# A 2048-point convolution and an MLP on one core: right-angle twisted transform with uniform tables, operands laid out by the host, and one list schedule for the whole kernel

## The chip, the cores and the metric

The program runs on one core of one Trainium2 chip. The metric is device time in microseconds (us) of one execution. Most executions of one kernel here lie within about 1% of its median; each run is classed as fast or slow by its time. The profile is one execution; its span is somewhat shorter than the time measured for the same run (238.2 and 240.03 us for the changed kernel).

PE is the matmul engine, PEld its weight load, DVE the vector engine, ACT the activation engine, POOL the general-purpose engine, SP the engine whose queue issues nearly all DMAs. PE writes its results into PSUM; an evacuation is the copy of such a result to SBUF, the memory that the other operands lie in, by DVE or ACT. `kv` is also called u.

## The reference, cut to what matters

```
x = A_q                                    # (2048, 512), bf16
q = layernorm(x)
kv = shift4(A_k, A_shift_k) * A_v          # 4-tap causal filter per channel, times v
y  = causal_conv(kv, A_ssm_k) + kv * A_ssm_D   # 2048-tap filter per channel, by FFT in fp32
h  = x + q * y
b  = layernorm(h)
h1 = gelu(layernorm(b) @ w1)               # 512 -> 512
x1 = b + shift_tokens(h1, -1, +1, -2, +2 by quarter of the channels) @ w2
out = h + x1 + gelu(layernorm(x1) @ w3) @ w4   # 512 -> 1792 -> 512
```

Both kernels compute the convolution as matmuls, in two steps of a Cooley-Tukey transform each way. Step 1 multiplies with small 32-row tables; an exchange between partitions (DMA, SBUF to SBUF) follows; step 2 has one table for each of 16 slices; the product of the two spectra is taken slice by slice; then the two inverse steps follow, with a second exchange between them. So the work has a neck: no token of `h` exists before the last slice of the inverse's first half has been exchanged. Below, "the transform" is all before that, "the norm stage" is the stretch after it in which layer norms, w1 and w2 work their way in, and "the MLP" is the rest (w3 and w4).

## The kernel before

The filter comes as (channel, time) and is transposed on PE; k is transposed by DMA; the transform's order is written by hand, and only what follows it is ordered by the list scheduler (`Plan`). This simulates the kernel with an estimated duration for each task: of the tasks that are ready it takes the one that can start first, at a tie the one of higher priority, and puts it on the engine that ends it first where there is a choice. The priorities are searched for in 40 rounds.

```
    for c in range(DC):
        nc.sync.dma_start(hnat[:, c, :], A_ssm_k[c * P:(c + 1) * P, :])
    for c in range(DC):
        nc.sync.dma_start_transpose(kT[:, c, 16:KW], k_r[:, c * P:(c + 1) * P])
    ...
    for c in range(DC):                    # 64 transposes of the filter, 8 evacuations
        for bh in range(2):
            pt = ps_c.tile([P, 8, P], BF16, name="pt", tag="pk")
            for j in range(8):
                nc.tensor.transpose(pt[:, j, :], hnat[:, c, 8 * bh + j:S:16], ident[:])
            evac(xh[:, 8 * bh:8 * bh + 8, c * P:(c + 1) * P], pt[:], 1024, ...)
    ...
    for bl in range(NL):                   # filter: step 1, exchange
        for h in range(4):
            step1([xh[:, 4 * bl + bq, :] for bq in range(4)], zch, bl, h)
        exchange(zh, zch, bl)
    for g in range(2):
        nc.sync.dma_start(q_sb[:, 8 * g:8 * g + 8, :], q_r[:, 8 * g:8 * g + 8, :])
    ...
    for b in range(NB):                    # by hand: shift, step 1 of kv, step 2 of the filter, q statistics
        xk[b] = shift(b)                   # 16 matmuls of 128 columns, then DVE: times v
        if b >= 4:
            bl, h = divmod(b - 4, 4)
            step1([xk[4 * bl + bq][:] for bq in range(4)], zck, bl, h)
            if h == 3:
                exchange(zk, zck, bl)
        if b >= 6:
            spectrum(ng)                   # step 2 of the filter: 4 matmuls and an evacuation
            ng += 1
        if b in (9, 13):
            tables(b // 4)                 # PE transposes of the inverse's tables
        if b >= 4:
            qstat(b - 4)
    ...
    for i in range(NH + 2):                # step 2 of kv, products, inverse's first half
        if i < NH:
            prs[i] = fwd(i)
        if i >= 2:
            inv(i - 2, prs[i - 2])
    ...
    plan = Plan(...)                       # from here on a list schedule: inverse's second half,
                                           # norms, w1, w2, w3 (pieces of 512 tokens), w4
```

## Time and profile before

| | us | read from |
|---|---|---|
| time, median of 2 runs | 268.1 | runs |
| transform, to the first 32-row inverse matmul | 109.1 | chain of waits |
| from there to the first matmul of w3 | 48 | instructions of w3's line: first at 156.9 |
| w3, w4 and the rest | 110 | the rest of the span |

The page of the kernel before: the busy line, and the span in 40 slices of 6.7 us (a digit is the busy share in tenths, PEclk the clock granted to PE).

```profile
span 266.8 us, 4530 instructions
PE 231.9 (87%) x1803; PEld 119.0 (45%) x1803; DVE 161.9 (61%) x323; ACT 143.3 (54%) x202; POOL 54.1 (20%) x101
...
PE   8665957999579988665988999999999999999994
...
DVE  7986807669927998299999994898022250013322
ACT  3638152788479998266867856556500046632000
...
PEclk9999995999959999796899999999999999999999
```

From the 24th slice on PE is full and its clock whole. Before that PE is not full for long; DVE is, from the 18th to the 24th slice (the norm stage). The same as a table of stretches; the columns are the stretch, its length, then for PE, PEld, DVE, ACT and POOL the busy us and in brackets the instructions, then granted clock, DMA share and GB/s.

```profile
0.00:40.00 40.00, 28.12 (x342) 17.57 (x343) 27.06 (x51) 19.64 (x21) 8.35 (x28) 1.00 0.98 313
40.00:80.00 40.00, 33.50 (x383) 19.37 (x384) 27.55 (x54) 27.01 (x33) 3.15 (x2) 0.84 0.28 110
80.00:109.00 29.00, 24.69 (x186) 7.44 (x182) 25.47 (x37) 26.46 (x29) 2.44 (x4) 0.97 0.47 168
109.00:157.00 48.00, 39.22 (x361) 24.36 (x362) 41.59 (x103) 31.76 (x55) 30.86 (x52) 0.90 0.24 86
157.00:268.00 111.00, 106.41 (x537) 50.24 (x534) 40.20 (x79) 38.42 (x65) 9.30 (x15) 0.99 0.06 20
```

In the first 80 us DVE and ACT, which empty every matmul's result out of PSUM, are each busy between half and 70% of the time. The chain of waits (start, length, what) says why around 40 us: the exchange of the filter, then the load of q queued behind it, then DVE's statistics of q, and behind those, in DVE's own order, the work that PE waits for.

```profile
26.56 6.07 DMA rd<-rc
...
32.65 7.34 DMA q_sb<-in_A_q_dram
...
40.01 0.70 DVE qst L414
...
41.55 1.86 PE pk L406 x16
...
105.58 3.46 DMA ra<-vst
...
109.09 3.30 PE mm L549 x31
```

The last two lines are the neck: the last exchange and the first inverse matmul with 32 rows.

### The profile page before, as it was taken

How to read it: one execution, taken by the hardware profiler on the slowest of the kernel's cores; microseconds unless marked ns; L12 is line 12 of the kernel's file. 1: busy time of each engine (PE TensorE's matmuls, PEld its weight loads, DVE VectorE, ACT ScalarE, POOL GpSimd, SP SyncE). 2: the span in 40 equal slices, each digit the busy share in tenths (PEclk: the TensorE clock that was granted, in tenths of full speed). 3: DMA queues.
4: the chain of work that ended last, by engine and by line, in shares of the span. 5: the costliest groups of instructions: out<-in, count | busy, mean ns of one | idle time of the engine just before them, and what ended most of it. 6: DMA issues, size and time to landing. Idle time of an engine off the chain costs nothing.

```text
span 266.8 us, 4530 instructions
## 1 busy us (share of the span) xinstructions
PE 231.9 (87%) x1803; PEld 119.0 (45%) x1803; DVE 161.9 (61%) x323; ACT 143.3 (54%) x202; POOL 54.1 (20%) x101
## 2 busy tenths in 40 slices
PE   8665957999579988665988999999999999999994
PEld 3522834555242222224655756445444444444441
DVE  7986807669927998299999994898022250013322
ACT  3638152788479998266867856556500046632000
POOL 3503000000130102029998442251000000000000
PEclk9999995999959999796899999999999999999999
DMA  7999990340701465891000000000011110000111
GB/s 241 249 271 360 407 346 37 142 160 15 295 11 41 153 241 179 295 396 39 1 2 0 4 0 0 2 1 0 2 39 39 39 39 2 0 20 20 42 39 39
DMA packets 18791, 28.08 MB, mean 105 GB/s; under 512 B 10065, under 2 KB 13906, under 8 KB 17234
## 3 DMA queue, kind: packets, MB, share of 16 engines
q1 hardware_dynamic: 17952, 26.74, 29.0%
q0 software_dynamic: 288, 1.05, 1.3%
q8 instruction: 14, 0.23, 0.4%
q10 hardware_dynamic: 530, 0.01, 0.1%
q14 instruction: 7, 0.06, 0.1%
HBM read 11.02 MB, written 2.10 MB: 49 GB/s over the span
## 4 chain that ended last, share of the span: by engine, by line
PE 57%; DVE 24%; DMA 6%; ACT 5%; POOL 4%; issue 2%; ACTq 0%; POOLq 0%
PE mm L717 18%; PE mm L702 18%; DVE st L566 4%; PE pk L406 4%; PE mm L662 3%; DVE rd L571 3%; DMA q_sb<-in_A_q_dram 3%; DMA rd<-rc 2%; DVE rt L315 2%; PE psg L396 2%; DVE vst L342 2%; ACT rc L339 2%; PE psk L396 2%; PE psva L484 2%; DVE pr L474 1%
## 5 line engine op out<-in xcount | busy, mean ns | idle before, releaser
L708 ACT ACTIVATE ra<-mm 128x512 bf16<-128x512 f32 x56 | 33.4, 597 | 49.7 <-PE mm L702 49.6
L702 PE MATMUL mm<-rc,rb 128*128 128x512 bf16 x224 | 50.8, 379 | 0.0
L717 PE MATMUL mm<-rt,ra 128*128 128x512 bf16 x224 | 49.0, 379 | 0.0
L725 DVE TENSOR_TENSOR ob<-mm,rd 128x512 bf16<-128x512 f32 x16 | 11.1, 692 | 61.4 <-PE mm L717 61.4
L717 PEld LDWEIGHTS <-ra 128*128 128x128 bf16 x224 | 22.0, 98 | 26.4
L702 PEld LDWEIGHTS <-rb 128*128 128x128 bf16 x224 | 21.6, 98 | 24.8
L406 PE MATMUL pk<-diag,rb 128*128 128x128 bf16 x256 | 19.8, 238 | 4.4 <-DVE xk L409 4.3
L406 PEld LDWEIGHTS <-rb 128*128 128x128 bf16 x256 | 18.3, 150 | 8.8 <-issue 7.5
L637 PE MATMUL mm<-rc,rf 128*128 128x256 bf16 x128 | 17.8, 295 | 0.0
L530 ACT COPY rc<-ptx 128x512 bf16<-128x512 bf16 x26 | 14.6, 583 | 4.6 <-PE ptx L623 4.6
L662 PE MATMUL mm<-rf,rb 128*128 128x512 bf16 x64 | 16.2, 380 | 1.0 <-ACT rb L643 0.9
L339 ACT CAST asb<-psk 128x1024 bf16<-128x1024 f32 x16 | 16.1, 1030 | 0.5 <-ACT asb L339 0.4
L571 DVE SCALAR_TENSOR_TENSOR rd<-q_sb,qmv,z 128x512 bf16<-128x512 bf16 x16 | 12.7, 792 | 4.6 <-ACT z L560 4.6
L414 DVE BATCH_NORM_STATS2 qst<-q_sb 128x6 f32<-128x512 bf16 x16 | 10.9, 680 | 6.5 <-DMA q_sb<-in_A_q_dram 6.5
L409 DVE TENSOR_TENSOR xk<-pk,rb 128x512 bf16<-128x512 f32 x16 | 10.9, 681 | 6.3 <-PE pk L406 6.2
L560 ACT ACTIVATE z<-mm,qrs 128x512 f32<-128x512 f32 x16 | 10.6, 697 | 7.4 <-PE mm L549 5.7
L637 PEld LDWEIGHTS <-rf 128*128 128x128 bf16 x128 | 13.2, 106 | 2.3
L667 DVE SCALAR_TENSOR_TENSOR q_sb<-rd,cr,mm 128x512 bf16<-128x512 bf16 x16 | 11.7, 733 | 3.7 <-PE mm L662 3.7
L396 PE MATMUL psg<-rd,rf 128*64 128x512 bf16 x64 | 10.3, 418 | 4.2 <-ACT rd L339 4.0
L396 PEld LDWEIGHTS <-rf 128*64 128x64 bf16 x128 | 5.7, 115 | 17.2 <-issue 16.2
L473 DVE TENSOR_TENSOR pr<-asb,rd 128x1024 bf16<-128x1024 bf16 x16 | 11.0, 687 | 3.5 <-ACT asb L339 3.5
L339 ACT CAST rd<-psg 128x1024 bf16<-128x1024 f32 x13 | 13.0, 1028 | 0.0
(224 smaller groups left out, 347.2 us busy)
## 6 DMA issues: line engine op xcount, KB each, us to landing
rd<-rc SPq DMA_DIRECT2D x16, 256.0 KB, 6.0
rc<-ra SPq DMA_DIRECT2D x16, 256.0 KB, 2.4
ra<-vst SPq DMA_DIRECT2D x16, 256.0 KB, 2.4
ra<-in_A_ssm_k_dram SPq DMA_DIRECT2D x4, 512.0 KB, 5.1
rb<-in_A_v_dram SPq DMA_DIRECT2D x2, 1024.0 KB, 8.0
q_sb<-in_A_q_dram SPq DMA_DIRECT2D x2, 1024.0 KB, 8.3
out_dram<-ob SPq DMA_DIRECT2D x16, 128.0 KB, 1.8
rb<-in_B_w_dram SPq DMA_DIRECT2D x1, 1792.0 KB, 7.3
```

What stands on the lines that cost most here:

```text
L339: nc.scalar.copy(o, i)
L396: nc.tensor.matmul(ps[64 * t:64 * t + 64, r, :], lhsT=ftab[:, kh, r, t, :], rhs=z[:, kh, t, :], start=True, stop=True)
L406: nc.tensor.matmul(pk[:, c * P:(c + 1) * P], lhsT=kT[:, c, 16 + b - j:KW - 16 + b - j + 1:16], rhs=diag[:, c, j, :], start=(j == 0), stop= ...
L530: nc.scalar.copy(o, i)
L571: nc.vector.scalar_tensor_tensor(out=h_sb[:, b, :], in0=q_sb[:, b, :], scalar=qmv[:, b, 0:1], in1=tl["z", b][:], op0=SUB, op1=MUL)
L637: nc.tensor.matmul(pw_[:, j * 256:(j + 1) * 256], lhsT=w1_sb[:, k, m * P:(m + 1) * P], rhs=hnT[:, k, p * 256:(p + 1) * 256], start=(k == 0 ...
L662: nc.tensor.matmul(px[:], lhsT=shifted(m, b), rhs=w2_sb[:, m, :], start=(m == 0), stop=(m == DC - 1))
L667: nc.vector.scalar_tensor_tensor(out=x1[:, b, :], in0=hbm[:, b, :], scalar=tl["cr", b // 2][:, b % 2:b % 2 + 1], in1=tl["x", b][:], op0=MU ...
L702: nc.tensor.matmul(pg[:], lhsT=w3_sb[:, k, fc * P:(fc + 1) * P], rhs=lnT[:, k, g * 512:(g + 1) * 512], start=(k == 0), stop=(k == DC - 1))
L708: nc.scalar.activation(gbuf[:, g % 2, fc, :], tl["g", g, fc][:], ACT.Gelu_apprx_tanh)
L717: nc.tensor.matmul(po[:], lhsT=gbuf[:, g % 2, fc, i * P:(i + 1) * P], rhs=w4_sb[:, fc, :], start=(fc == 0), stop=(fc == FC - 1))
L725: nc.vector.tensor_tensor(out=ob[:], in0=tl["o", 4 * g + i][:], in1=xh1[:, b, :], op=ADD)
```

## The change

Its intent:

- The transform is formulated anew (odd frequencies, a "right-angle" twist), so that all 16 slices have tables of one form. They are computed by Sin on ACT where they are needed; the 33 PE transposes that turned them and the special cases of slice 0 go.
- The host lays out k (already transposed, in blocks) and the filter (as time by channel). The 64 PE transposes and the DMA-transposes go. The shift's 256 matmuls of 128 columns become 112 of 128 to 512 columns, with the same columns in total.
- All 8 PSUM banks are one pool, and one list schedule orders the whole kernel, DMAs included, with a model of when a transfer lands.
- The exchange moves in halves, slices are taken in an order (`KO`) whose first 12 are all that 24 of the 32 matmuls of an inverse block need, and the inverse's second half starts on those for two of its four blocks.
- w3 is taken in pieces of 256 tokens. POOL no longer applies normalisations to blocks; it still computes their factors. In the norm stage a sum and its statistics are now two tasks of the plan instead of one.

The diff, cut to its core; cuts are marked with `...`.

```
 class Plan:
-    def __init__(self, pools, rounds=40):
+    LEAD = 1.5
+    TAIL = 0.7
+    def __init__(self, rounds=40, seed=1):
...
+            if t["move"]:
+                stream = max(stream, at + self.LEAD) + t["move"]
+                done[n] = stream + self.TAIL
...
-    for c in range(DC):
-        nc.sync.dma_start(hnat[:, c, :], A_ssm_k[c * P:(c + 1) * P, :])
-    for c in range(DC):
-        nc.sync.dma_start_transpose(kT[:, c, 16:KW], k_r[:, c * P:(c + 1) * P])
+    for g in range(4):
+        task(("ld_x", g), {"Q": 0.5}, dma(xh[:, 4 * g:4 * g + 4, :], x_r[:, 4 * g:4 * g + 4, :]), move=1.5, ...)
+        task(("ld_k", g), {"Q": 0.5}, dma(rk[:, kgo[g]:kgo[g + 1]], A_k[:, kgo[g]:kgo[g + 1]]), ...)
...
+    def isin(r, neg, m, slot):             # the inverse's tables, for all slices at once
+        def f(e, _):
+            for a in range(4):
+                nc.scalar.activation(tv[:, m, :, a, slot, :], xi[r]..., ACT.Sin, bias=..., scale=...)
...
+                for j in [4 * g] + [x for x in range(4 * g - 3, 4 * g + 4) if x != 4 * g]:
+                    b0, b1 = max(4 * g, j), min(4 * g + 3, j + 3)
+                    nc.tensor.matmul(ps[:, bs[i], (b0 - 4 * g) * P:(b1 + 1 - 4 * g) * P], lhsT=kcols(j, c),
+                                     rhs=diag[:, c, b0 - j:b1 + 1 - j, :]..., ...)
...
+                task(k, {"PE": 0.5}, step1(k, x, bl, hp), dp, take=2)
+                task(("e1" + nm, bl, hp), E1024, evac(k, zc[:, bl, 2 * hp:2 * hp + 2, :]), drop=k)
...
+    KO = [4 * a + b for b in range(4) for a in range(4)]
...
+        task(("ld_q", g), {"Q": 0.5}, dma(q_sb[...], q_r[...]), ["C", "S", "NC", "NS", ("fs", 0), ("fs", 1)] + XU[:4], move=1.5)
...
+        if bl < 2:
+            task(("I0", bl), {"PE": 1.5}, inv1(bl, range(6), 0), dp + [("xA", kh) for kh in KO[:12]] + ..., take=4, many=4)
+            task(("I", bl), {"PE": 0.5}, inv1(bl, (6, 7), 1), [("I0", bl)] + INVX)
...
-                task(("hb", c), {"V": 0.42, "G": 0.92, "A": 0.8}, hbf(c), [("rr", p)])
+                task(("hb", c), {"V": 0.43, "A": 0.82}, hbf(c), [("rr", p)])
...
-    for g in range(4):
-        bs = order[4 * g:4 * g + 4]
-        for fc in range(FC):
-            task(("M", g, fc), {"PE": 0.87}, w3mm(g, fc), ...)
+    for g in range(8):
+        bs = order[2 * g:2 * g + 2]
+        for fp in range(FC // 2):
+            task(("M", g, fp), {"PE": 0.9}, w3mm(g, fp), ...)
...
+    a["A_ssm_k"] = a["A_ssm_k"].T          # on the host; k is cut into blocks and transposed there too
```

## The prediction

> **What bounds the kernel now.** The page gives a span of 266.8 us. The chain of waits has three parts. (1) Transform, 0 to 109 us: nothing is saturated. By five-microsecond windows PE is busy 28 us of the first 40, DMA share near 1.0 (DMA-transposes of k, filter load, exchange); DVE idles 6.5 us until q lands at 40 us, and its in-order queue stalls PE behind it (granted clock then 0.53). From 80 to 105 us DVE and ACT are 82 to 100% busy. (2) Layer norms, 112 to 145 us: DVE is 95% busy, PE loses about 8 us idle and 3 us to a low clock. (3) MLP: from 157 to 263 us PE never stops, 216 ns per 512-column matmul. Its work can't shrink.
>
> **Removed.** 64 filter transposes with 8 evacuations (5.4 us PE, 6.7 us ACT and DVE; step 1 starts only at 14.5 us); four DMA-transposes; 33 table transposes (2.8 us PE) and their evacuations (about 6 us); a 5.8 us int16 add on DVE before step 1. The shift's 256 matmuls of 128 columns become 112 wider ones: 1.15 us per block to about 0.9, 4 us of PE.
>
> **Added.** Sin tables: about 9 us of ACT, 5 of DVE, 6 of POOL, estimated from the 2.0 us Sin of 2048 elements; mostly in the first 35 us. POOL no longer takes normalisations, so DVE and ACT get 10 us more in the norm stage; in return DVE's subtract-multiply of h should lose its 1.2 us outliers (median 0.74). The Trainium skill's "GPSIMD Engine Reference", specifications table, says GpSimd shares SBUF interfaces with VectorE; the two durations agree but don't prove it.
>
> **Unchanged.** 80 evacuations of 1024 columns (ACT 1.02, DVE 1.22 us), 32 products (0.69), three exchanges of 4.2 MB. w3 goes to 448 matmuls of 256 columns; w1 has that form, 16 in 1.75 us, so no cost.
>
> **Critical path.** The transform becomes DMA-bound, then evacuation-bound. Filter, k and v (6.3 MB) and two exchanges (8.4 MB) must pass before the second half of step 2 on u: at the 360 to 400 GB/s of undisturbed slices about 40 us, so step 2 of u starts near 42 us. Then 32 evacuations, 32 products and the q statistics remain, about 70 us of DVE and ACT work, 35 if shared evenly, 42 at the packing seen here. Last exchange 3 us: the 32-row inverse starts near 88 us instead of 109, a gain of 21. After it, before took 157.7 us. The norms stay DVE-bound, but starting two of four inverse blocks on 12 of 16 slices and taking w3 in 256-token pieces should fill 5 to 7 us of PE's holes: about 151 us.
>
> 88 + 151 = 239, plus 1 us between span and time: **240 us**, 230 to 251 for 8 in 10. Chances: faster by over 2% 0.95, within 2% 0.04, slower 0.01.
>
> **What the profile would show.** Right: first 32-row inverse matmul at 83 to 94 us; PE busy about 10 us less in total; 147 to 154 us from there to the end; w3's matmuls near 108 ns apart; DVE over 90% busy before the inverse and in the norms. Wrong: exchanges landing after 50 us, PE waiting long on DMA, the inverse after 95 us, or DVE at 100% in the norms with PE idle over 12 us.
>
> **What would make it wrong.** In-order queues, DMA's above all, holding a planned order that the chip doesn't keep; the larger norm load giving back the gain; weight loads not hidden under 256-column matmuls; or a schedule that packs better than 85%, with 225 to 230 as the floor that PE's own work sets.

## The result

The changed kernel takes 240.1 us (median of 2 runs, 240.03 and 240.25), against 268.1 us before; the ratio is 0.896, with an interval of 0.882 to 0.910. A ratio is computed as the mean time of one kernel's fast runs over that of the other's in the same rounds, so it isn't quite the ratio of the medians. The prediction of 240.0 holds to 0.1 us, which is luck to some part: the changed kernel's own runs later spread over 239.2 to 242.2. By the letter, the first 32-row inverse matmul starts at 82.9 us, just before the 83 to 94 that were named, since 24 matmuls of the first block now run ahead of the neck. The table takes the first one that waits for the last exchange, as the prediction's 88 us did.

| | before | after | predicted |
|---|---|---|---|
| transform, to the last slices' inverse matmul, us | 109.1 | 87.0 | 88 |
| from there to the end of the span, us | 157.7 | 151.2 | 151 |
| PE busy, us | 231.9 | 214.2 | about 10 less |
| first w3 matmul after the inverse started, us | 48 | 34 | |

The page after: 22.1 us of the 28.6 us of span were won in the transform, 6.5 behind it.

```profile
span 238.2 us, 4553 instructions
PE 214.2 (90%) x1786; PEld 127.9 (54%) x1786; DVE 162.4 (68%) x330; ACT 139.2 (58%) x203; POOL 44.3 (19%) x87
...
PE   7589998876978948799999999999999999999994
...
DVE  6986779998999989999999993451168961020121
ACT  3799637798999935978687273163231543516300
...
PEclk9999999999999976999999999999999999999998
```

The stretches after, with the same borders:

```profile
0.00:40.00 40.00, 33.46 (x370) 17.32 (x371) 31.13 (x54) 27.76 (x41) 15.82 (x29) 1.00 0.76 286
40.00:80.00 40.00, 32.88 (x272) 13.53 (x272) 38.19 (x59) 36.52 (x39) 1.91 (x4) 1.00 0.82 278
80.00:109.00 29.00, 22.18 (x237) 12.09 (x233) 27.17 (x69) 20.15 (x34) 11.46 (x22) 0.88 0.34 113
109.00:157.00 48.00, 48.00 (x371) 33.71 (x372) 38.51 (x98) 26.93 (x46) 12.45 (x26) 1.00 0.04 12
157.00:268.00 111.00, 77.69 (x542) 51.25 (x540) 27.44 (x54) 27.85 (x46) 2.68 (x6) 0.98 0.04 15
```

The sum of DVE's work is the same as before (162 us), and ACT's nearly so. What differs is where it stands: between 40 and 80 us DVE and ACT are now busy 38.2 and 36.5 us of 40, where they were 27.6 and 27.0. PE's clock is whole up to 80 us.

The chain of waits after:

```profile
18.23 14.05 PE ps L513 x112
32.31 1.23 DVE rv L522
...
49.10 8.35 DMA r<-r
...
57.49 0.64 PE ps L572 x4
...
84.19 2.72 DMA r<-rk
...
87.04 1.09 PE ps L648 x8
```

Line 513 is the shift: 14 us of PE in one piece. `r<-r` at 49.1 us is the last exchange of kv's step 1, which stands in the queue behind q and lands at 57.5 us. `r<-rk` is the last exchange before the neck.

### The profile page after: what moved, and what is told of

Its sections match the earlier page's. It is cut to its first block, busy times and chain, and to the rows that moved or that the text cites. A ratio compares the mean times of both kernels' runs of the same rounds, so it can differ in the third digit from the quotient of the medians.

```text
span 238.2 us, 4553 instructions
## 1 busy us (share of the span) xinstructions
PE 214.2 (90%) x1786; PEld 127.9 (54%) x1786; DVE 162.4 (68%) x330; ACT 139.2 (58%) x203; POOL 44.3 (19%) x87
## 4 chain that ended last, share of the span: by engine, by line
PE 71%; ACT 10%; DVE 9%; DMA 7%; issue 2%; POOL 1%; DVEq 0%; ACTq 0%
PE ps L793 21%; PE ps L809 20%; PE ps L513 6%; PE ps L753 6%; PE ps L595 6%; DVE r L293 5%; PE ps L728 5%; ACT r L291 4%; DMA r<-r 4%; PE ps L714 3%; PE ps L648 2%; DMA rs<-in_A_ssm_k_dram 2%; ACT rk L291 2%; ACT zr L653 2%; PE ps L572 1%
## 5 line engine op out<-in xcount | busy, mean ns | idle before, releaser
L799 ACT ACTIVATE r<-ps 128x512 bf16<-128x512 f32 x56 | 33.2, 598 | 46.5 <-PE ps L793 46.2
L793 PE MATMUL ps<-rt,rv 128*128 128x256 bf16 x448 | 52.0, 273 | 0.0
L809 PE MATMUL ps<-rs,r 128*128 128x512 bf16 x224 | 50.0, 379 | 0.0
L291 ACT CAST r<-ps 128x1024 bf16<-128x1024 f32 x44 | 42.4, 1033 | 12.9 <-PE ps L530 10.4
L793 PEld LDWEIGHTS <-rv 128*128 128x128 bf16 x448 | 43.6, 98 | 7.1
L809 PEld LDWEIGHTS <-r 128*128 128x128 bf16 x224 | 21.8, 98 | 24.6
L293 DVE CAST r<-ps 128x1024 bf16<-128x1024 f32 x20 | 24.1, 1220 | 2.6 <-PE ps L530 1.4
L572 PE MATMUL ps<-r,rt 128*64 128x512 bf16 x128 | 18.3, 384 | 4.5 <-ACT r L291 1.7
L587 DVE TENSOR_TENSOR rs<-r,r 128x1024 bf16<-128x1024 bf16 x32 | 20.0, 684 | 0.1
L753 PE MATMUL ps<-rk,r 128*128 128x512 bf16 x64 | 16.3, 379 | 0.1
L572 PEld LDWEIGHTS <-rt 128*64 128x64 bf16 x128 | 7.2, 108 | 15.3 <-issue 11.3
L291 ACT CAST rk<-ps 128x1024 bf16<-128x1024 f32 x14 | 13.5, 1024 | 1.2 <-PE ps L595 0.9
L513 PE MATMUL ps<-diag,rk 128*128 128x256 bf16 (+3 forms) x112 | 14.1, 288 | 0.0
L728 PEld LDWEIGHTS <-rk 128*128 128x128 bf16 x128 | 12.3, 98 | 2.9 <-issue 1.0
```

Source lines behind the costliest of these rows:

```text
L291: nc.scalar.copy(o, i)
L293: one(e).tensor_copy(o, i)
L513: nc.tensor.matmul(ps[:, bs[i], (b0 - 4 * g) * P:(b1 + 1 - 4 * g) * P], lhsT=kcols(j, c), rhs=diag[:, c, b0 - j:b1 + 1 - j, :].rearrange(" ...
L572: nc.tensor.matmul(ps[64 * t:64 * t + 64, bs[r], :], lhsT=ftab[:, kh, t, r, :], rhs=z[:, kh, t, :], start=True, stop=True)
L587: one(e).tensor_tensor(out=pr[:, s, a, :, :], in0=zu[:, kh, :, :], in1=g, op=MUL)
L728: nc.tensor.matmul(ps[:, bs[0], j * 256:(j + 1) * 256], lhsT=w1_sb[:, k, m * P:(m + 1) * P], rhs=hnT[:, p % HN, k, :], start=(k == 0), sto ...
```

## The experiments

Every time below is a median; "the standard" is the changed kernel, 240 us. The first run repeats it. The runs were made on four chips: 9 (after_again, before_layout, after_noearly, after_noqs), 4 (after_late, after_w3_512, after_noqs_replan, after_warm), 13 (after_fifo, after_poolprod, after_qearly) and 11 (after_s1dep). The standard was repeated on chip 9 only. The kernel before ran in each call, and its fast runs have medians of 266.0 to 267.9 us, so 1 or 2 us between runs of different calls can be the chip's.

### The standard, again (after_again)

No edit.

> The changed kernel unaltered, as the standard for the others of this call: 240 us, inverse's late slices at 87 us. It has no rival; if it differs by over 1 us from the recorded 240.1, smaller differences of the other runs aren't read.

Measured: 239.98 us (239.21 to 242.17). The four runs show a mean granted clock of 0.977, 0.993, 0.979 and 0.990 with 242.17, 239.21, 240.73 and 239.24 us, in that order: the spread goes with the clock. The two profiles of the same program show how. First the standard's stretches from 10 to 20 us, then those of this run:

```profile
10.00:15.00 5.00, 3.39 (x64) 1.44 (x57) 5.00 (x7) 4.95 (x7) 4.01 (x4) 1.00 1.00 402
15.00:20.00 5.00, 4.64 (x55) 2.37 (x55) 3.14 (x4) 4.79 (x7) 3.31 (x3) 1.00 1.03 411
```

```profile
10.00:15.00 5.00, 3.04 (x60) 1.31 (x52) 5.00 (x5) 4.86 (x6) 4.39 (x5) 0.91 1.01 407
15.00:20.00 5.00, 4.62 (x56) 1.95 (x49) 3.58 (x5) 3.75 (x5) 2.92 (x2) 0.75 1.03 412
```

The third figure from the end is the clock: 1.00 in the one, 0.75 in the other. The inverse's late slices then start at 87.04 and 89.26 us, and the spans are 238.2 and 240.4. So nothing under about 2 us is read from single runs here, and traces are compared with an eye on the clock of their first 20 us.

### The kernel before with the host's layout alone (before_layout)

```
-        nc.sync.dma_start(hnat[:, c, :], A_ssm_k[c * P:(c + 1) * P, :])
-        nc.sync.dma_start_transpose(kT[:, c, 16:KW], k_r[:, c * P:(c + 1) * P])
-            (64 transposes of the filter and their evacuations)
+        nc.sync.dma_start(xh[:, 4 * g:4 * g + 4, :], x_r[:, 4 * g:4 * g + 4, :])
+        nc.sync.dma_start(kT[:, c, 16:KW], A_k[c * P:(c + 1) * P, :])
```

> The kernel before, but k and the filter come laid out by the host: no DMA-transpose, no 64 PE transposes, nothing else changed. Theory (the gain of the transform is mainly packing: tables off the front of DVE, one order for all engines): the int16 add on DVE still holds step 1 until about 12 us and q still lands late, so 259 to 265 us, 3 to 9 us of the 28. Rival (the layout is the gain): 252 us or less.

Measured: 264.2 us (263.6 to 264.5), 0.994 of the kernel before (interval 0.986 to 1.002). The interval includes no gain at all. In the trace, step 1 starts at 12.3 us instead of 14.5 and the inverse at 104.2 instead of 109.1 (PE's timeline below), but the rest takes 158.2 us, as before.

```profile
104.22 2.50 PE L543 MATMUL mm<-ra,f 32*128 32x512 bf16 x24 [1.62 <-DMA ra<-vst]
```

So the transposes, which take PE time, DMA time and evacuations, were mostly not what the transform waited for. The 259 to 265 us of the theory hold, and the rival that the layout is the gain falls. One thing may hide a little of the layout's worth: with the transposes gone PE idles 6.7 us before step 1, and its clock from 10 to 15 us is 0.50, where it was 1.00.

### The same work in a plain greedy order (after_fifo)

```
-        prio = top = self.first()
+        prio = top = {t["n"]: -t["n"] for t in self.t}
...
-ROUNDS = 40
+ROUNDS = 1
```

> The changed kernel's work, tables and data layout unaltered, but the plan is greedy in the order in which the tasks are written, without priorities by what follows and without the 40 rounds of search. Theory (most of the gain is packing: layout alone gave before only about 4 us): 8 to 14 us slower, 248 to 254. Rival (what was removed gives the gain, any sensible order will do): within 4 us of 240.

Measured: 258.4 us (257.5 to 259.7), ratio to before 0.967. It is more than I expected: 18 us slower than the standard, with the same 1786 matmuls on data of the same layout. The rest isn't quite the same: the planner also chooses engines, and here DVE has 337 instructions and 168.4 us of work, ACT 196 instructions, against 330, 162.4 and 203. The inverse's late slices start at 93.7 us (6.7 later than in the standard, but 15.4 earlier than in the kernel before), and from there to the end it takes 162.0 us: 10.8 longer than in the standard and 4.3 longer than in the kernel before, which had a searched plan in this stage already. The first matmul of w3 comes 58 us after the inverse started, against 34. These are the late slices in PE's timeline and its stretches from 93 us to the first w3 at 152 us:

```profile
93.70 0.61 PE L648 MATMUL ps<-r,f 32*128 32x512 bf16 x8 [2.58 <-DMA r<-rk]
```

```profile
93.00:108.00 15.00, 11.43 (x104) 5.23 (x104) 14.09 (x37) 9.49 (x16) 8.06 (x12) 0.77 0.39 124
108.00:152.00 44.00, 35.91 (x289) 22.86 (x290) 41.64 (x114) 24.55 (x41) 16.58 (x34) 1.00 0.00 1
```

DVE is full (41.6 of 44 us) while PE idles 8 us. DVE works in the list's order: the statistics of the second layer norm, which w3 waits for, begin at 130.9 us, when those of the first are done with all 16 blocks (the last at 129.2). In the standard they begin at 114.2 us, with the first norm's going on until 126.2, and are spread until 189.9. So a full engine is no sign of a good order.

### The early start of the inverse: one run that missed (after_noearly), one that did it (after_late)

The first attempt emitted the early part together with the late part:

```
             bs = tl["I", bl]
-            for x in xs:
+            if len(xs) == 6:
+                return
+            for x in range(8):
```

> The changed kernel with the same plan, but the early parts of the first two inverse blocks are emitted together with their last slices, after the last exchange. Theory as predicted (early start and 256-token pieces fill 5 to 7 us together): about 2 to 3 us slower, 242 to 243. Rival, from the trace: before the landing only 24 matmuls of one block run, about 1.9 us of PE; after it DVE is the engine that is full, so 0.5 to 1.2 us slower.

Measured: 241.5 us (240.1 to 241.8). It tests nothing: the trace still shows 24 matmuls of the first block before the last exchange lands, since each matmul waits for its own slices and they are first in the order. So its 1.5 us over the standard, in the same call, are a measure of what nearly the same program can differ by.

The second run turns the order round:

```
-            for x in xs:
-                    ... start=(x == 0), stop=(x == 7)
+            if len(xs) == 6:
+                return
+            for x in (6, 7, 0, 1, 2, 3, 4, 5):
+                    ... start=(x == 6), stop=(x == 5)
```

> The early start of the inverse truly undone (the run before left it in place, because each matmul waits for its own slices): for the first two blocks the last slices' matmuls come first, so all 32 of a block wait for the last exchange; plan unchanged. Rival from the trace: 24 matmuls, 1.9 us of PE, move behind the landing at 87 us: 1.5 to 2.5 us slower than 240.0, a cold clock included. My prediction's share for it (half of 5 to 7 us) would be 2.5 to 3.5. If within 0.7 us: DVE or the later stage absorbs it.

PE's timeline of the standard, then of this run (start, length, line, shapes; in brackets how long it was idle before and for what):

```profile
82.89 1.87 PE L648 MATMUL ps<-r,f 32*128 32x512 bf16 x24
87.04 1.04 PE L648 MATMUL ps<-r,f 32*128 32x512 bf16 x8 [2.28 <-DMA r<-rk]
```

```profile
87.84 3.39 PE L650 MATMUL ps<-r,f 32*128 32x512 bf16 x32 [4.13 <-DMA r<-rk]
```

Measured: 243.6 us (242.0 to 243.9), 3.6 us slower. The idle time of PE grew from 2.3 to 4.1 us, and its 32 matmuls then took 3.4 us: 31 of these take 1.9 us elsewhere in both traces. The granted clock from 87 to 92 us is low in both (0.66 here, 0.50 in the standard). The landing itself comes 0.8 us later here, and from there to the end the profile is 2.6 us longer. So 1.9 us of work moved behind the landing cost about 2.6 to 3.6 us, on another chip than the standard's. That is about what the prediction's share for it said (2.5 to 3.5), and at or over the rival's 2.5.

### w3 in pieces of 512 tokens again (after_w3_512)

```
-    for g in range(8):
-        bs = order[2 * g:2 * g + 2]
-        for fp in range(FC // 2):
+    for g in range(4):
+        bs = order[4 * g:4 * g + 4]
+        for fc in range(FC):
```

(with two buffers of 512 tokens in place of four of 256, and 224 matmuls of 512 columns in place of 448)

> w3 taken again in pieces of 512 tokens (224 matmuls of 512 columns, two buffers), a new plan by the same search. Theory as predicted (256-token pieces fill PE's holes in the norm stage): 2 to 4 us slower, with PE idle between 115 and 140 us. Rival (all holes lie before 108 us, before any piece of w3 can be ready): within 1.5 us of 240.

Measured: 241.6 us (241.0 to 243.0), 1.6 us slower, with a new plan. The expected holes between 115 and 140 us aren't there: from 108 to 126 and from 126 to 140 us PE is busy 17.8 of 18 and 13.9 of 14 us, although w3 starts only at 126.0 us instead of 121.0. This is less than the smaller of the theory's two numbers and about what other new plans of the same work differ by (240.9 and 242.3 us below). The pieces' own gain isn't settled; it is small.

### Without the statistics of q, in the old plan (after_noqs) and in a new one (after_noqs_replan)

Wrong numbers; the work downstream stays the same.

```
-            nc.vector.bn_stats(qst[:, b, :], q_sb[:, b, :])
+            if b == 0:
+                nc.vector.bn_stats(qst[:, b, :], q_sb[:, b, :])
-            nc.vector.bn_aggr(qmv[:, b, :], qst[:, b, :])
+            nc.vector.bn_aggr(qmv[:, b, :], qst[:, 0, :])
```

> Wrong on purpose: 15 of the 16 statistics of q aren't taken (10 us less DVE work between 51 and 88 us), plan and order unchanged. Theory (from 41 us on the transform is bound by DVE and ACT): 2 to 5 us faster, 235 to 238, with the late inverse slices at 82 to 85 us. Rival (bound by exchange traffic or by PE's chain): under 1 us, and the inverse still at 86 to 87.

Measured: 241.5 us (240.5 to 243.4), not faster; inverse's late slices at 87.3 us. With the plan frozen, only DVE is relieved, and ACT is as full as before (19.2 of 20 us between 60 and 80).

The second run leaves out all 16 and tells the planner (`{"V": 0.9}` becomes `{"V": 0.2}`):

> Wrong on purpose: none of q's 16 statistics is taken and the plan is made anew knowing it, so evacuations can move from ACT to the freed DVE. Theory (DVE and ACT together bound the transform; with the plan frozen only DVE was relieved and ACT stayed full): the late inverse slices at 81 to 84 us, 235 to 238 us. Rival (exchanges and the chain bound it): inverse still at 86 to 88, 239 to 241.

Measured: 239.6 us (239.4 to 241.0); its output is wrong. The inverse's late slices start at 86.2 us. By the numbers this is the rival's. Two things temper it. Half of the 16 statistics of the standard run between 81.8 and 88.1 us, in the wait for the last exchange; where they are left out, DVE stands idle instead (busy 8.2 of 15 us from 80 to 95 us in the run with the old plan, 13.7 in the standard). And this run's profile has the low clock in its first 41 us (0.96), as the repeated standard has, whose inverse started at 89.3; against that one it is 3.0 us earlier, where half of the other eight statistics' 5.3 us (8 at 0.66) would make 2.7. One pair of profiles isn't proof. What is sure is that 11 us less of DVE's work bring the whole kernel less than 2 us.

### Keeping PE's clock up in the last gap (after_warm)

```
+                def keep(e, bs):
+                    for i in range(10):
+                        nc.tensor.matmul(ps[:, bs[0], :], lhsT=wup[:, 0:P], rhs=wup[:], start=True, stop=True)
+                task("dm0", {"PE": 2.2}, keep, [("I0", 0)], take=1)
```

> 10 idle matmuls of 512 columns put between the early and the late slices of the first inverse block, where PE waits 2.3 us for the last exchange and the granted clock falls to 0.65 in 85 to 95 us. Theory (the spread from 239.2 to 242 follows the clock): clock 1.0 there and 1 to 2 us faster, 238 to 239, less spread. Rival (DVE holds the norms, PE's clock there is free): within 0.7 us of 240.

Measured: 244.2 us (244.0 to 245.7), 4 us slower. The clock from 80 to 95 us is 1.00 as intended (0.77 in the standard), and it helps nothing: the late slices start at 89.5 us, and from there it takes 152.7 us, not less than 151.2. The start may be late because the added task made another plan, and its profile too has the low clock early (0.96 in the first 41 us). How much of the 4 us is which stays open; that PE's clock at the start of the norm stage costs the kernel time isn't supported.

### Products on POOL (after_poolprod)

```
-            task(("p", kh, a), {"V": 0.7}, prod, ...)
+            task(("p", kh, a), {"V": 0.7, "G": 2.3}, prod, ...)
```

> The plan may put a product of 1024 columns on POOL (estimated 2.3 us from POOL's 1.13 us for 512 columns); it takes 6 of the 32. Theory (DVE and ACT bound the stretch from 41 to 84 us, so relief of 4 us of DVE that stays useful in the plan moves the inverse): inverse's late slices 1 to 3 us earlier, 237.5 to 239. Rival (POOL and DVE get in each other's way at SBUF): DVE's products beside them over 0.75 us instead of 0.68, POOL's over 2.5, 240 or slower.

Measured: 246.7 us in the five fast runs (246.6 to 248.9; a sixth, of 250.5, was slow, and the median of all is 247.5), ratio to before 0.925 where the standard has 0.90. The plan is a new one. The inverse's late slices start at 94.3 us, 7 us late. First DVE's, then POOL's timeline of one place:

```profile
68.49 0.69 DVE L587 TENSOR_TENSOR rs<-r,r 128x1024 bf16<-128x1024 bf16 x1
69.10 1.22 DVE L293 CAST r<-ps 128x1024 bf16<-128x1024 f32 x1
70.24 3.22 DVE L587 TENSOR_TENSOR rs<-r,r 128x1024 bf16<-128x1024 bf16 x2
```

```profile
70.34 5.09 POOL L587 TENSOR_TENSOR rs<-r,r 128x1024 bf16<-128x1024 bf16 x2
```

A product takes DVE 0.69 us alone. When POOL has one in hand (2.55 us), two of DVE take 3.22 us, the time of one of POOL's and one of DVE's: one of them, it seems, waits until POOL's is done. The maximum of DVE's 26 products is 2.62 us. Together the 26 take 24.6 us, 6.8 more than at 0.686 us each, which is more than the 4.1 us of the six that were taken off. DVE's busy time rose from 162.4 to 170.0 us; the rest of that is other work that runs longer or that the new plan put there. The rival holds.

### q earlier (after_qearly), the filter's step 1 before the shift (after_s1dep)

```
-... ["C", "S", "NC", "NS", ("fs", 0), ("fs", 1)] + XU[:4], move=1.5)
+... ["C", "S", "NC", "NS", ("fs", 0), ("fs", 1)], move=1.5)
```

> q is loaded once the tables have left its memory, in the gap of 28 to 36 us in which DMA is idle, instead of ahead of the last exchange of u. Theory (the last exchange, which lands at 57.5 us behind q and which the chain of waits shows with 8 us, holds the transform): landing near 52, inverse at 83 to 85, 237 to 239. Rival (evacuations hold it; statistics of q now compete with step 1 of u instead): landing earlier but inverse within 1 us of 87, 239 to 241.

Measured: 242.3 us (241.3 to 244.4). q is loaded from 23.7 us on, the last exchange of kv is issued by 50.7 us with no load of q before it, and the inverse's late slices start at 86.6 us, 0.5 us earlier. So the 8 us of DMA in the chain of waits were no cost that removing could win: from 41 to 84 us DVE and ACT are as full without it (80.9 of 86 us, 80.6 in the standard). The new plan did more than was asked: DMA is busy between 25 and 35 us (share 0.93, 0.38 in the standard) and step 2 starts at 34.3 us instead of 41.2, which didn't move the inverse either. The two starts in PE's timeline:

```profile
34.27 0.62 PE L572 MATMUL ps<-r,rt 128*64 128x512 bf16 x4
...
86.57 0.61 PE L648 MATMUL ps<-r,f 32*128 32x512 bf16 x8 [2.44 <-DMA r<-rk]
```

The edit of the second run:

```
+                task(("sh", g, cp), ..., dp + ... + ([("s1h", bl, hp) for bl in range(4) for hp in range(4)] if g >= 2 else []), take=2)
```

> The second half of the shift's matmuls has to follow the filter's step 1 on PE; in the changed kernel 14 us of shift run in one piece from 18 to 32 us, the filter's last step 1 comes after it, DVE and ACT run short of work (12 of 20 us busy between 25 and 35 us) and DMA is idle from 28 to 36. Theory (this shortage, not DMA or the statistics of q, is what is left to gain in the transform): filter's exchange landed by 31 us, DMA idle under 4 us, step 2 starting by 38 instead of 41, inverse's late slices at 83 to 85, 237 to 239. Rival (the gap only moves, since DVE and ACT have the same work): inverse at 86 to 89, 239 to 242.

Measured: 240.9 us (240.5 to 242.3), inverse's late slices at 87.5 us. The filter's step 1 does end early (the last at 23.2 us), but step 2 still starts at 41.2 us, and DVE and ACT are as short of work between 25 and 35 us (11.3 of 20 us). So the shortage stayed, and this run doesn't test whether it is what's left to gain. The run with q earlier does: there DMA was busy in that stretch and step 2 started 7 us earlier, and the inverse still came at 86.6 us. By that the theory falls.

No version tried here beats the changed kernel; the best medians, 239.6 for a wrong result and 240.0 for the standard itself, are the same.

## Why the prediction was right, and where it was not

**The time and its split: right.** Predicted 240, measured 240.1; the inverse predicted at 88 us, measured at 87.0; the rest predicted at 151 us, measured at 151.2. That the split fits so well is luck in part, as the next point shows.

**"The transform becomes DMA-bound, then evacuation-bound": the sum was right, its terms weren't.** I took the exchanges to be through at 42 us, with 70 us of DVE and ACT work left, packed at 83%. The exchange of kv landed at 57.5 us, which I had named as a sign of being wrong. Two errors cancel. The stretch from 41 to 84 us, before and then after:

```profile
41.00:84.00 43.00, 37.04 (x405) 20.29 (x404) 29.94 (x58) 30.82 (x37) 3.15 (x2) 0.85 0.25 100
```

```profile
41.00:84.00 43.00, 36.06 (x305) 15.07 (x302) 41.01 (x65) 39.54 (x42) 3.07 (x6) 1.00 0.79 270
```

DVE and ACT together do 80.6 us of work there, not 70: step 2 of the filter too only starts at 41.2 us, so its 16 evacuations are in it, while half of q's statistics have been put off. But they do it at 94% (80.6 of 86 us) where before reached 71%, and 83% was assumed. The plain order of after_fifo reaches 78% in the same stretch (67.2 of 86). 70 over 0.83 and 80.6 over 0.94 make nearly the same (84 and 86 us of two engines). DMA alone didn't hold the first 41 us either: near full from 5 to 20 us, its share is 0.00 between 30 and 35 us, at the end of PE's 14 us of shift.

**Which part of the change gave it: open for the most part.** The prediction listed the removals first and named the planned order only as a risk. The layout alone gives the old kernel 0 to 4 us (4.9 in the transform by the trace). Without priorities and search the changed kernel loses 18 us, 6.7 in the transform and 10.8 behind it. The 10.8 can't be a share of the gain: the change won only 6.5 us there, and the kernel before had a searched plan in that stage already. They say what such a plan is worth, not what this change added. In the transform even the plain order starts the inverse 15.4 us before the old order, written by hand. So of the 22.1 us there 6.7 are shown for priorities and search, at most 4.9 for the layout and about 10 for neither; what tables, wider shift, half exchanges and the common list of all engines share of them wasn't separated. Nor are these clean shares, since each part makes room for the others.

**"Evacuation-bound" as a cause: not shown.** The engines are full, but relieving DVE of 11 us brought the inverse at most 3 us and the kernel less than 2. In the run with q earlier all of q's statistics were begun by 82.2 us (87.3 in the standard), and the inverse came only 0.5 us sooner. When POOL's products made DVE's 26 take 6.8 us longer, the inverse came 7 us later; but that was another plan, in which ACT had less to do (32.1 us from 41 to 84, 39.5 in the standard), so it doesn't show the cause either.

**PE's busy time: mis-sized.** About 10 us less was predicted, 17.7 measured. The transposes were 8.2 as costed. The shift's busy time fell from 19.8 to 14.1 us, 5.7 instead of 4, and the sum in the prediction was rounded down from 12. The remaining 3.8 I put down to the clock, without a run that isolates it: the granted clock was 0.85 from 41 to 84 us before and 1.00 after. The Trainium skill's "TensorE: Matmul & The Clock Gate" (Part 1, "What's actually happening") says that the throttled state is the default and that activity releases it; PE's clock before fell where PE had idled (0.53 after the wait for q), so the trace agrees. The prediction didn't count it as a gain.

**"Starting early and 256-token pieces fill 5 to 7 us of PE's holes": right in sum, not in shares.** The stage gained 6.5 us. The early start is worth about 2.6 to 3.6 us by itself, the pieces at most 1.6, within what one plan differs from another. PE's idle time from the inverse to the first w3 fell from 8.8 us (of 48) to 4.6 (of 34).

**w3's 256-column matmuls: right.** 56 take 6.11 us, 109 ns each, so 448 of them cost what 224 of 216 ns did.

**POOL off the norms: right in direction, small.** DVE's subtract-multiply of h had two outliers of 1.20 us among 16 and has none (maximum 0.75 us): 0.9 us in all. Both began while POOL had a normalisation in hand (at 124.1 us, POOL's until 124.8; at 139.7, POOL's until 140.4), and the experiment with products on POOL shows the same contention. The price was as predicted: DVE and ACT take 17.5 us of normalisations instead of 8.0, and the stage became shorter all the same.

## What to carry to other kernels

When no engine is full and yet everything waits, try what the order alone is worth, by planning the same work in a poorer order: here a searched plan against a plain one was 18 us, and the operations that looked dear (transposes) were worth 4 at most. But such a test says what the plan is worth now, not what the change added: for that, look stage by stage at what the old kernel had. Read a long DMA in the chain of waits as a question, not as a cost: moving it away won nothing, and the engines behind it were as full as before. And before giving an idle POOL a tensor-tensor operation to relieve DVE, look at what DVE does at that moment: it can lose more than it hands over (6.8 us for 4.1 here).

## What the Trainium skill lacked or had wrong

- "SBUF — State Buffer", section "SBUF: two separate sides", calls the port pair that GpSimd and VectorE share an exclusive lock. The runs agree and add the size: a DVE product of 1024 columns went from 0.69 to as much as 2.62 us beside a POOL product of 2.55 us, and the new plan that moved six of 32 products to POOL was 6.7 us slower than the standard's 240, fast runs with fast runs. "GPSIMD Engine Reference" (section 1, Specifications) names the contention for instructions with two SBUF inputs without a size.
- "TensorE: Matmul & The Clock Gate", Part 1, gives the condition for a throttled clock as an idle window of about 3.4 us. Here the clock fell to 0.75 on average from 15 to 20 us in one of two profiles of the same program, with no gap of PE longer than 1.5 us in the 10 us before, only 2.7 and 3.0 us of busy time in each 5. The page's "A second HAM failure mode" describes such re-throttling by short gaps. The two spans differ by 2.2 us. No page says which busy share keeps the clock up, and these runs give none: over 10 us, 57% did not keep it here and 60% did not in after_noqs_replan (both 5 to 15 us), while 62% did in the other profile and 59% in the kernel before (10 to 20 us).
- None has a figure for what the order of the same work is worth; here a greedy plan in written order against a searched one was 258.4 against 240.0 us.
